# Closing lists: rows turned in blocks of 32 on VectorE by way of DRAM, and a search on the eight largest scores

## The chip, the cores and the metric

One core of a Trainium2 chip runs the kernel. The metric is the time of one execution on the device, in microseconds. Three runs of the kernel before took 1522.15, 1522.92 and 1523.63 us: median 1522.92.

## The reference

Two stages follow each other. The first mixes x [8, 2496, 256] along the sequence: a real Fourier transform over the 2496 rows, a complex 256 x 256 product with bias, soft thresholding by 0.01, and the inverse transform. Its 8 x 2496 = 19968 rows of 256 are the tokens of the second stage, in which each of eight experts takes exactly 2496 tokens:

```
logits = x @ w_gate                        # 19968 x 8
for idx in argsort(-logits.flatten()):     # greedy, largest score first
    tok, e = idx // 8, idx % 8
    if assigned[tok] >= 0 or counts[e] >= 2496: continue
    assigned[tok] = e; counts[e] += 1
out[mask_e] = relu(x[mask_e] @ w1[e]) @ w2[e]      # 256 -> 1024 -> 256, for each expert
```

## The kernel before

**Stages.** The first part (`phase_a`) does the transforms batch by batch and leaves the rows in the DRAM tensor `YD` and the logits in `LG`. While its last batches run, each expert gets an early list of 512 tokens that are sure to be its own (`Router.early`), from the first four batches. After the logits of all batches are in, eight closing lists follow (`Router.closing`, i = 0 to 7): list i finds the expert that fills up next, and the remaining 1984 of its tokens are computed. Its later tokens then move to their next best expert, so that list i+1 can only be searched once list i is found.

**Search of a closing list.** `H.m` holds each token's best score among the `no` = 8 - i experts that are open, 156 tokens to each of 128 partitions; `AG` and `EQ` say whose it is. The wanted score is the one at which the fullest expert has 2496 tokens. `count` (line 445) does one count: for each threshold and each pair of experts one VectorE instruction compares 156 columns and sums (line 454), two small ones part the two experts of a pair (lines 458, 459), and two small matmuls add up over the partitions (lines 464, 465). Lists 0 and 1 use `bisect` (line 495) behind one count: 19 halvings, and a last count, 21 rounds. Lists 2 to 6 use `search` (line 470) with three thresholds a round, 11 rounds and a last count. Each round waits for the result of the one before. List 7 takes what is left.

**A list's work.** `lists` (line 522) turns the marks into row numbers, by matmuls (line 551) and ScalarE. `Experts.load` fetches the expert's weights by the number found, with indirect DMAs of GpSimd (line 617), and splits them into two parts each. `Experts.run` (line 630) gathers tiles of 128 rows from `YD` with indirect DMAs (line 640), two tiles to a buffer `xg`. A chunk is four tiles, 512 tokens; a closing list has four chunks, 16 tiles. `xpose` (line 645) turns a chunk: for each half of the 256 columns TensorE transposes four 128 x 128 blocks into a PSUM bank (line 655), ScalarE copies the bank as the high part (line 658), and VectorE subtracts it for the low part (line 659):

```
for q in range(nt):
    t = 4 * c + q
    T.transpose(ps.t[:, 128 * q:128 * q + 128], xg[t // 2].t[:, t % 2, 128 * m:128 * m + 128], H.idn)
```

`ffn1` (line 670) multiplies with W1 in three terms, eight groups of 128 of the hidden 1024; `ffn2` (lines 689 to 692) multiplies with W2; ScalarE and VectorE merge the two parts (lines 698, 699), and GpSimd scatters the rows to the output (line 702).

**Order.** Nothing is in program order by itself: `Plan.run` simulates five queues (TensorE, VectorE, ScalarE, GpSimd and SP) with costs from the code, takes at each step the task that can start first, then the one of lower `pos`, and emits the instructions in that order. Buffers come from rings or from groups of slots. `Q`, `SLACK`, `LATE` and `GAP` are its numbers: positions of stages, allowances for waits, and transfer times. A flag `fail` is raised if the certificates of the lists don't hold; then a slow general pass (`general`) computes all again behind a `tc.If`.

## Time and profile before

| | us |
|---|---|
| median of three runs | 1522.92 |
| profiled execution | 1523.78 |
| its span, first to last instruction | 1522.0 |
| TensorE busy | 1486.1 |
| VectorE busy | 1184.8 |
| ScalarE busy | 893.2 |
| GpSimd busy | 526.4 |

PE is TensorE's matmuls, PEld its weight loads, DVE is VectorE, ACT ScalarE, POOL GpSimd and SP the queue that issues plain DMAs. A busy time is the time in which at least one instruction of the engine was under way; instructions overlap, so the mean duration of one is longer than the step from one to the next. `x4` is a number of instructions. In a name such as `b<-h_idn,yst` the output stands first; buffers are shared slots, so one tile bears many names over the run. A bracket at the end of a row is idle time before the instruction and what ended it.

### The profile page before, as it was taken

To read this page: it belongs to the slowest core of one execution; us is meant where nothing else is said; L and a number is where in the kernel's file an instruction comes from. 1 tells how busy PE (TensorE), PEld (TensorE's weight loads), DVE (VectorE), ACT (ScalarE), POOL (GpSimd) and SP (SyncE) were. 2 spreads that over 40 slices of the span, in tenths; PEclk is the share of its full clock that TensorE was granted. 3 is DMA by queue.
4 is the path that set the end of the run, shared out by engine and by line. 5 is a ranking of instruction groups with operands and counts; after the bars stand their busy time and mean duration, and the time that the engine had idled before them with its cause. 6 is when DMAs were issued, how large, how long until landed. Compare 5 with 4: busy or idle time off the path is not lost.

```text
span 1522.0 us, 33650 instructions
## 1 busy us (share of the span) xinstructions
PE 1486.1 (98%) x9511; PEld 1248.3 (82%) x9514; DVE 1184.8 (78%) x3981; ACT 893.2 (59%) x2092; POOL 526.4 (35%) x497
## 2 busy tenths in 40 slices
PE   8999999999999999999999999999999999999997
PEld 6878888888888867888777888878888888888886
DVE  5868888776898968899999999999787875543432
ACT  4668999899899785445535344363536355442331
POOL 0013424334323445312523525244433525442112
PEclk9999999999999999999999999999999999999999
DMA  5598788787777675423212212121312223220000
GB/s 199 182 298 260 231 273 269 227 279 238 239 226 246 187 222 159 155 89 119 85 42 87 66 56 91 42 93 58 99 50 86 71 68 106 68 70 29 20 25 29
DMA packets 134959, 206.98 MB, mean 136 GB/s; under 512 B 26942, under 2 KB 96747, under 8 KB 134763
## 3 DMA queue, kind: packets, MB, share of 16 engines
q1 hardware_dynamic: 114793, 146.42, 30.7%
q0 software_dynamic: 19840, 58.22, 11.9%
q8 instruction: 77, 1.26, 0.4%
q14 instruction: 119, 0.97, 0.2%
q10 hardware_dynamic: 130, 0.11, 0.0%
...
## 4 chain that ended last, share of the span: by engine, by line
PE 79%; DVE 9%; DMA 4%; ACT 4%; issue 2%; SPq 1%; POOL 0%; POOLq 0%; ACTq 0%; DVEq 0%
PE b L670 23%; PE b L689 14%; PE b L690 7%; PE b L1144 6%; PE b L1173 4%; PE b L1125 3%; PE b L1152 3%; PE pt L670 3%; PE b L1211 3%; PE b L1085 3%; DVE junk L454 2%; PE pt L689 2%; PE b L1231 2%; PE b L655 2%; PE pt L690 1%
## 5 line engine op out<-in xcount | busy, mean ns | idle before, releaser
L955 POOL TENSOR_TENSOR s2l<-s2c,s2h 120x512 fp32r<-120x512 f32 (+1 forms) x84 | 106.6, 1274 | 248.1 <-ACT s2h L952 235.8
L454 DVE SCALAR_TENSOR_TENSOR junk<-h_m,st,h_AG 128x156 bf16<-128x156 f32 (+1 forms) x472 | 155.7, 376 | 2.1
L702 POOL DMA_INDIRECT out_dram<-xTh,li x64 | 67.8, 1060 | 210.8 <-DVE xTh L699 108.7
L1144 PE MATMUL b<-wt,xTh 128*128 128x256 f32 x640 | 130.0, 300 | 3.5 <-ACT xTh L1131 3.5
L1144 PEld LDWEIGHTS b<-wt,xTh 128*128 128x128 f32 x640 | 103.1, 192 | 9.6 <-ACT xTh L1131 3.7
L1242 POOL TENSOR_TENSOR yTl<-yr,yTh 128x468 bf16<-128x468 f32 (+1 forms) x55 | 62.3, 1132 | 121.6 <-ACT yTh L1238 92.4
L702 POOL DMA_INDIRECT out_dram<-xTl,li x64 | 65.5, 1023 | 104.0 <-DVE xTl L699 54.0
L1144 PE MATMUL b<-wt,xTl 128*128 128x256 f32 x320 | 92.5, 289 | 2.9 <-DVE xTl L1134 2.4
L1125 PE MATMUL b<-FG,sh 128*128 128x128 f32 x640 | 89.8, 277 | 1.2 <-DVE sh L1106 1.2
L1125 PEld LDWEIGHTS b<-FG,sh 128*128 128x128 f32 x640 | 83.1, 191 | 8.5 <-issue 2.7
L1173 PE MATMUL b<-y,FG 64*128 64x256 f32 x640 | 80.3, 390 | 0.0
L698 ACT COPY xTh<-b 128x256 f32<-128x256 f32 x58 | 21.7, 375 | 93.0 <-PE b L690 75.9
L1173 PEld LDWEIGHTS b<-y,FG 64*128 64x128 f32 x640 | 58.3, 186 | 14.9 <-issue 3.2
L1157 DVE TENSOR_TENSOR y<-b,sx 128x512 f32<-128x512 f32 x80 | 54.8, 685 | 18.0 <-ACT sx L1155 17.5
L955 DVE TENSOR_TENSOR xl<-xt,xh 117x512 fp32r<-117x512 f32 (+1 forms) x77 | 56.6, 745 | 15.0 <-ACT xh L952 14.4
L1211 PE MATMUL b<-s2h,d 120*117 120x512 f32 (+1 forms) x168 | 66.6, 403 | 0.0
L1144 PEld LDWEIGHTS b<-wt,xTl 128*128 128x128 f32 x320 | 61.3, 191 | 5.7 <-DVE xTl L1134 4.6
L698 ACT COPY xTl<-b 128x256 f32<-128x256 f32 x74 | 27.8, 376 | 63.8 <-PE b L690 50.6
L1085 PE MATMUL b<-xh,d 117*120 117x512 f32 (+1 forms) x154 | 62.8, 421 | 1.0 <-ACT xh L952 1.0
L1152 PE MATMUL b<-wt,xTh 128*128 128x256 f32 x320 | 62.4, 287 | 0.0
L1236 DVE TENSOR_TENSOR yr<-b,yTh 128x468 f32<-128x468 f32 (+1 forms) x88 | 54.7, 622 | 7.9 <-ACT yTh L1235 4.3
L699 DVE TENSOR_TENSOR xTl<-b,xTl 128x256 f32<-128x256 f32 x74 | 30.9, 418 | 36.1 <-ACT xTl L698 33.7
...
## 6 DMA issues: line engine op xcount, KB each, us to landing
...
```

The lines of the kernel that those rows point to most:

```text
L454: v(cols + 59, p, lambda k=k: V.scalar_tensor_tensor(junk[k % 2].t[:, 0:cols], H.m[:, 0:cols], c.t[:, k // ng:k // ng + 1], ag(k % ng)[:, ...
L670: T.matmul(ps.t[:, 0:w], lhsT=W1[m].t[:, a, 128 * ft:128 * ft + 128], rhs=x_.t[:, 0:w], start=q + m == 0, stop=q + m == 3)
L689: T.matmul(ps.t, lhsT=hh.t[:, u:u + 128], rhs=W2[ft // 4].t[:, :, ft % 4], start=ft == 0, stop=False)
L690: T.matmul(ps.t[:, 0], lhsT=hl.t[:, u:u + 128], rhs=w_[0], start=False, stop=ft == 7)
L702: ins = P.indirect_dma_start(out=self.out, out_offset=bass.IndirectOffsetOnAxis(ap=oi.t[0:M, oo + t:oo + t + 1], axis=0), in_=o.t[0:M], in ...
L955: lambda: eng.tensor_tensor(lb[1](), src(), hb[1](), op=OP.subtract), [srcb, hb[0]], [lb[0]], port=True)
L1085: T.matmul(ps.t[0:M], lhsT=d1[0:k_, a, 0:M], rhs=v.t[0:k_], start=i == 0, stop=i == 2)
L1125: T.matmul(ps.t[:, :, dt, i], lhsT=sh[k // 8].t[:, k % 8, 128 * dt:128 * dt + 128], rhs=at(Ft, k), start=True, stop=True)
L1144: T.matmul(pc.t[:, c], lhsT=a.t[:, 1 - c, dt], rhs=wt[2 - c].t[:, w, dt], start=not pb and dt == 0 and a is th and w == 0, stop=(c == 1 or ...
L1152: T.matmul(pa.t, lhsT=a.t[:, 2, dt], rhs=wt[0].t[:, w, dt], start=dt == 0 and a is th and w == 0, stop=dt == 1 and a is tl)
L1173: T.matmul(ps4[i].t[:, r], lhsT=at(Gt, 2 * (p - 1 + r) + c)[h], rhs=zs[r].t[h, c], start=c == 0, stop=c == 1)
L1211: T.matmul(ps.t[0:M, gs_], lhsT=d5[0:k_, a, 0:M], rhs=v.t[0:k_, gs_], start=i == 0, stop=i == 2)
```

## The change

In all eight closing lists the rows are turned otherwise. Behind the gather of two tiles, SP writes both (256 rows) to a DRAM buffer `XG` and reads them back in four loads into `xw`: partition 32G + r gets, for each block of 32 rows, row r's columns 64G to 64G + 63. `xturn` then takes the place of `xpose`: for each half, two VectorE instructions transpose all 32 x 32 blocks of a pair (256 columns each) into an SBUF tile `xf`, ScalarE copies it as the high part, and VectorE subtracts. The 256 columns of a row now stand in another order on the partitions, so the rows of W1 are fetched with indices in that order (two more columns in `wi`). The early lists keep `xpose`.

The search is otherwise too. List 0 makes one count, five halvings and a count at the upper end, and then calls `few`. Lists 1 to 6 extrapolate from the last list's counts to two thresholds, at 0.5 and 0.85 of the way, count both in one round, take the better as upper end, and call `few`. There VectorE takes, for each open expert and partition, the eight largest scores under the upper end (three instructions of 156 columns an expert), and then 7 rounds (6 in list 0) with seven thresholds each: one comparison of 7 x no x 8 elements, one sum over the eights, one matmul over the partitions, and small instructions. A last count with all tokens stands behind it as before. `search` is gone. A few small instructions keep the counts for the next list's extrapolation.

`Q`, `SLACK` and `P1X` have new values, so the order of all queues is another; the loads of one constant (`cD5`) are planned later; two small buffers share others' places. Inside the `tc.If`, `general` is planned with numbers of its own. The diff, without the lists of numbers:

```diff
+BLOCK = (0, 1, 2, 3, 4, 5, 6, 7)
...
+SN, SR = 7, 7
+FR = 0.5, 0.85
+NEAR = 5
+WIDE = 100.0
...
+def few(K, H, pos, hi, lo, nr, no, pk):
+
+    V, v, T = K.V, K.v, K.T
+    cand, sc, D, wq = K.sb("eq", [128, 8, 8]), K.sb("lo", [128, 4, NJ]), K.sb("cno", [128, 1]), K.sb("wq", [128, SR * SN])
     low, at = lo
+    at0 = lo[1]
+    v(1, pos(), lambda: V.tensor_tensor(D.t, hi.t[:, 0:1], at0(), op=OP.subtract), [hi, low], [D])
+    v(SN * nr + 59, pos(), lambda: V.tensor_scalar(wq.t[:, 0:SN * nr], H.sq[:, 0:SN * nr], D.t[:, 0:1], None, op0=OP.mult), [H.b_sq, D], [wq])
+    c = K.sb("st", [128, 8])
+    v(SN, pos(), lambda c=c: V.tensor_scalar(c.t[:, 0:SN], wq.t[:, 0:SN], at0(), None, op0=OP.add), [wq, low], [c])
+    v(NJ + 59, pos(), lambda: V.scalar_tensor_tensor(sc.t[:, 3], H.m, hi.t[:, 0:1], H.m, op0=OP.is_lt, op1=OP.mult), [H.b_m, hi], [sc])
+    for e in range(no):
+        v(NJ, pos(), lambda e=e: V.tensor_tensor(sc.t[:, e % 3], H.ML[:, e], sc.t[:, 3], op=OP.not_equal), [H.b_ML, sc], [sc])
+        v(NJ + 59, pos(), lambda e=e: V.scalar_tensor_tensor(sc.t[:, e % 3], sc.t[:, e % 3], GONE, H.ML[:, e], op0=OP.mult, op1=OP.add), [H.b_ML, sc], [sc])
+        v(NJ, pos(), lambda e=e: V.max(cand.t[:, e], sc.t[:, e % 3]), [sc], [cand])
+    n = SN * no
+    for k in range(nr):
+        G, cn, ps = K.sb("Sme", [128, SN, 8, 8], BF), K.sb("ge0", [128, SN, 8], BF), K.psum(pk, [128, SN, 8])
+        nn, mx, g8, sm, b, c2 = K.sb("RD", [128, SN, 8]), K.sb("g8", [128, 8]), K.sb("g8", [128, 8]), K.sb("any", [128, 1]), K.sb("cno", [128, 1]), K.sb("st", [128, 8])
+        v(8 * n, pos(), lambda G=G, c=c: V.tensor_tensor(G.t[:, :, 0:no].rearrange("p j e k -> p j (e k)"), cand.t[:, None, 0:no].rearrange("p a e k -> p a (e k)").to_broadcast([128, SN, 8 * no]), c.t[:, 0:SN, None].to_broadcast([128, SN, 8 * no]), op=OP.is_ge), [cand, c], [G])
+
+        def total(G=G, cn=cn):
+            with K.nc.allow_low_precision(reason="counts up to 8"): V.tensor_reduce(cn.t[:, :, 0:no], G.t[:, :, 0:no], op=OP.add, axis=AX.X)
+        v(8 * n, pos(), total, [G], [cn], port=False)
+        K.t(.1, pos(), lambda cn=cn, ps=ps: T.matmul(ps.t[:, :, 0:no], lhsT=H.ones, rhs=cn.t[:, :, 0:no], start=True, stop=True), [cn, H.b_ones], [ps], slack=SLACK['count'])
+        v(n, pos(), lambda ps=ps, nn=nn: V.tensor_tensor(nn.t[:, :, 0:no], ps.t[:, :, 0:no], hi.t[:, None, 1:1 + no].to_broadcast([128, SN, no]), op=OP.add), [ps, hi], [nn], slack=SLACK['back'])
+        v(n, pos(), lambda nn=nn, mx=mx: V.tensor_reduce(mx.t[:, 0:SN], nn.t[:, :, 0:no], op=OP.max, axis=AX.X), [nn], [mx], port=False)
+        v(80, pos(), lambda mx=mx, g8=g8, sm=sm: V.tensor_scalar(g8.t[:, 0:SN], mx.t[:, 0:SN], float(CAP), 0.0, op0=OP.is_ge, op1=OP.add, accum_out=sm.t), [mx], [g8, sm])
+        v(59, pos(), lambda k=k, sm=sm, b=b, at=at: V.scalar_tensor_tensor(b.t, sm.t, wq.t[:, SN * k:SN * k + 1], at(), op0=OP.mult, op1=OP.add), [sm, wq, low], [b])
         low, at = b, lambda b=b: b.t
+        if k < nr - 1: v(SN, pos(), lambda k=k, b=b, c2=c2: V.tensor_scalar(c2.t[:, 0:SN], wq.t[:, SN * k + SN:SN * k + 2 * SN], b.t[:, 0:1], None, op0=OP.add), [wq, b], [c2])
         c = c2
     return b
...
+                                                                          in_offset=bass.IndirectOffsetOnAxis(ap=wi.t[:, (2 + m if block and not k else m):(2 + m if block and not k else m) + 1], axis=0)), 524e3, [wi], [r], run=4096, late=LATE['raw'])
...
+            if block and (t % 2 or t == NT - 1):
+                h, n_ = t // 2, t % 2 + 1
+                XG, w = K.dram("XG", [256, 256]), K.sb("xw", [128, 8, 2, 32])
+                K.dma(pos_g(t) + Q['xw'], lambda g=g, XG=XG, n_=n_: K.nc.sync.dma_start(XG.t[0:128 * n_].rearrange("(t p) d -> p t d", p=128), g.t[:, 0:n_]), 131e3 * n_, [g], [XG])
+
+                def ld(w=w, XG=XG, n_=n_):
+                    for G in range(4):
+                        K.nc.sync.dma_start(w.t[32 * G:32 * G + 32, 0:4 * n_].rearrange("p t m c -> p t (m c)"), XG.t[0:128 * n_].rearrange("(t r) (G c) -> G r t c", r=32, G=4)[G])
+                plan.add('SP', 1.6, pos_g(t) + Q['xv'], ld, [XG], [w], load=moved(131e3 * n_, 256, late=LATE['sp']))
+                xg[h] = w
+
+        def xturn(c, pos):
+            nt = min(4, NT - 4 * c)
+            w_ = 128 * nt
+            xT[c] = [[K.sb("xT", [128, 512], F32R) for _ in range(2)] for _ in range(2)]
+            for m in range(2):
+                h, l = xT[c][m]
+                f = K.sb("xf", [128, 512])
+                for k in range((nt + 1) // 2):
+                    w, e = xg[2 * c + k], min(8, 4 * nt - 8 * k)
+                    v(32 * e, pos + .5 * m - Q['xv2'], lambda f=f, w=w, m=m, k=k, e=e: V.transpose(f.t[:, 256 * k:256 * k + 32 * e], w.t[:, 0:e, m]), [w], [f])
+                plan.add('A', .095 + w_ / 1200, pos + .5 * m, lambda f=f, h=h: A.copy(h.t[:, 0:w_], f.t[:, 0:w_]), [f], [h])
+                v(w_, pos + .5 * m, lambda f=f, h=h, l=l: V.tensor_tensor(l.t[:, 0:w_], f.t[:, 0:w_], h.t[:, 0:w_], op=OP.subtract), [f, h], [l])
...
-        xpose(0, base - Q['xp'])
+        turn = xturn if block else xpose
+        turn(0, base - Q['xp'])
...
-            rng, r = self.rng, RR[i]
-            v(1, pos(), lambda: V.tensor_tensor(rng.t, lohi.t[:, 0:1], lohi.t[:, 1:2], op=OP.subtract), [lohi], [rng])
-            if r > 1:
-                c = search(K, H, pos, (lohi, lambda: lohi.t[:, 1:2]), rng, r, N4, CAP, no, ag, NJ, "pq", self.junk, self.acc, eqs)
...
+            hi, cur = K.sb("hi", [128, 9]), K.sb("pv", [128, 24]) if i < 6 else None
+            if i:
+                pv = self.pv
+                v(2 * no, pos(), lambda pv=pv: V.copy_predicated(pv.t[:, 8:24].rearrange("p (a e) -> p a e", a=2)[:, :, 0:no], fp.t[:, None, 0:no].bitcast(I32).to_broadcast([128, 2, no]), pv.t[:, 8:24].rearrange("p (a e) -> p a e", a=2)[:, :, no:no + 1].to_broadcast([128, 2, no])), [fp, pv], [pv])
+                q8, dl, c, P, mx, lt = K.sb("g8", [128, 8]), K.sb("any", [128, 1]), K.sb("st", [128, 8]), K.sb("P2", [128, 2, 9]), K.sb("wi", [128, 2]), K.sb("fs", [128, 2])
+                v(67, pos(), lambda pv=pv, q8=q8: V.scalar_tensor_tensor(q8.t[:, 0:no], pv.t[:, 8:8 + no], float(CAP), pv.t[:, 16:16 + no], op0=OP.subtract, op1=OP.mult), [pv], [q8])
+                v(8, pos(), lambda q8=q8, dl=dl: V.tensor_reduce(dl.t, q8.t[:, 0:no], op=OP.min, axis=AX.X), [q8], [dl], port=False)
+                v(61, pos(), lambda dl=dl, c=c, pv=pv: V.scalar_tensor_tensor(c.t[:, 0:2], H.fr, dl.t[:, 0:1], pv.t[:, 0:1].to_broadcast([128, 2]), op0=OP.mult, op1=OP.add), [dl, pv, H.b_fr], [c])
+                v(9, pos(), lambda pv=pv, hi=hi: V.tensor_copy(hi.t[:, 1:1 + no], pv.t[:, 8:8 + no]), [pv], [hi])
+                v(1, pos(), lambda pv=pv, hi=hi: V.tensor_copy(hi.t[:, 0:1], pv.t[:, 0:1]), [pv], [hi])
+                v(2, pos(), lambda c=c, P=P: V.tensor_copy(P.t[:, :, 0], c.t[:, 0:2]), [c], [P])
+                ps = count(K, H, pos, c, no, ag, NJ, "pq", self.junk, self.acc, eqs, 2)
+                for h in range(2):
+                    w_ = (ng, n2)[h]
+                    v(16, pos(), lambda ps=ps, P=P, h=h, w_=w_: V.tensor_copy(P.t[:, :, 1 + ng * h:1 + ng * h + w_], ps.t[:, 2 * ng * h:2 * ng * h + 2 * ng].rearrange("p (j g) -> p j g", j=2)[:, :, 0:w_]), [ps], [P], slack=SLACK['back'])
+                v(16, pos(), lambda P=P, mx=mx: V.tensor_reduce(mx.t, P.t[:, :, 1:1 + no], op=OP.max, axis=AX.X), [P], [mx], port=False)
+                v(2, pos(), lambda mx=mx, lt=lt: V.tensor_scalar(lt.t, mx.t, float(CAP), None, op0=OP.is_lt), [mx], [lt])
+                for j in range(2): v(9, pos(), lambda j=j, P=P, lt=lt, hi=hi: V.copy_predicated(hi.t[:, 0:1 + no], lt.t[:, j:j + 1].bitcast(I32).to_broadcast([128, 1 + no]), P.t[:, j, 0:1 + no]), [P, lt], [hi])
+                c = few(K, H, pos, hi, (lohi, lambda: lohi.t[:, 1:2]), SR, no, "pq")
...
-                c = bisect(K, H, pos, c2, KB - 3 if i < 6 else KB - 2, CAP, no, ag, NJ, "pq", self.junk, self.acc, eqs)
+                lo = bisect(K, H, pos, c2, NEAR, CAP, no, ag, NJ, "pq", self.junk, self.acc, eqs)
+                up = K.sb("st", [128, 8])
+                v(1, pos(), lambda lo=lo, up=up: V.tensor_tensor(up.t[:, 0:1], lo.t, H.wk[:, NEAR - 1:NEAR], op=OP.add), [lo, H.b_wk], [up])
+                ps = count(K, H, pos, up, no, ag, NJ, "pq", self.junk, self.acc, eqs)
+                v(8, pos(), lambda ps=ps, hi=hi: V.tensor_copy(hi.t[:, 1:9], ps.t[:, 0:8]), [ps], [hi], slack=SLACK['back'])
+                v(1, pos(), lambda up=up, hi=hi: V.tensor_copy(hi.t[:, 0:1], up.t[:, 0:1]), [up], [hi])
+                c = few(K, H, pos, hi, (lo, lambda: lo.t), SR - 1, no, "pq")
...
-            v(1, pos() + 5, lambda: V.tensor_copy(lohi.t[:, 0:1], c.t), [c], [lohi])
+            if i < 6:
...
+                self.pv = cur
...
+        v(2, pw, lambda: V.scalar_tensor_tensor(wi.t[:, 2:4], H.iE[:, 0:2], 32.0, wb.t.to_broadcast([128, 2]), op0=OP.mult, op1=OP.add), [wb, H.b_iE], [wi])
...
+    GROUPS = dict(W=(8, slots("sp8", "sh8", "FG8")), raw=(2, slots("xt")), xg=(10, G2), xw=(5, G2), xf=(2, G2), hid=(20, G2), xT=(8, G2), os=(8, slots("xTh", "xTl")),
...
+            W = X.load(base - Q['ll'], wi=wi, block=i in BLOCK)
+            X.run(CAP - EN, base, W, gi, 0, gs, oi, 0, lambda t, base=base, i=i: base + Q['gs'] * (t // 4) - (Q['gl2'] if i in BLOCK else Q['gl']) + .1 * (t % 4), block=i in BLOCK)
```

## Rows read from the trace of the kernel before

**Rows 1.** Page of the profile, part 1: busy us, share of the span, instructions.

```profile
PE 1486.1 (98%) x9511; PEld 1248.3 (82%) x9514; DVE 1184.8 (78%) x3981; ACT 893.2 (59%) x2092; POOL 526.4 (35%) x497
```

**Rows 2.** Stretches: length, busy us (instructions) by engine, granted clock, DMA share, GB/s.

```profile
740.00:1100.00 360.00, 352.52 (x1965) 292.30 (x1964) 338.42 (x1606) 161.97 (x400) 147.72 (x144) 1.00 0.23 72
1100.00:1510.00 410.00, 410.00 (x2241) 348.79 (x2241) 236.36 (x788) 166.89 (x389) 140.69 (x142) 1.00 0.18 57
```

**Rows 3.** Waits of TensorE: who for whom, us in total, times, longest.

```profile
PE b L464 <- DVE cnt L459: 7.4, 8, 1.9
...
PE b L670 <- DVE y L659: 0.2, 1, 0.2
```

**Rows 4.** Chain of waits from 1000 us on: start, us, what.

```profile
1036.11 0.44 PE b L655 x4
...
1320.35 0.44 PE b L655 x4
...
1410.54 0.44 PE b L655 x4
```

**Rows 5.** Stretches, line 655 alone: length, PE busy, PEld busy, clock, DMA, GB/s.

```profile
740.00:1100.00 360.00, 17.78 (x118) 13.55 (x116) 1.00 0.23 72
1100.00:1510.00 410.00, 20.36 (x136) 16.49 (x136) 1.00 0.18 57
```

**Rows 6.** Timeline of TensorE at 1426 us: start, us, engine, line, operation.

```profile
1426.05 0.28 PE L690 MATMUL b<-sh,xl 128*128 128x256 f32 x1
1426.17 0.38 PE L655 MATMUL b<-h_idn,yst 128*128 128x128 f32 x2
...
1426.84 0.39 PE L670 MATMUL b<-s1st,sh 128*128 128x512 f32 x1
```

**Rows 7.** Timeline of TensorE at 694 us, a counting pair.

```profile
694.07 0.39 PE L670 MATMUL b<-s1st,sh 128*128 128x512 f32 x1
694.30 0.18 PE L464 MATMUL b<-cnt,h_ones 128*128 128x4 bf16 x1
...
694.68 0.28 PE L690 MATMUL b<-FG,y 128*128 128x256 f32 x1
```

**Rows 8.** Groups of VectorE: count, busy us, mean ns, idle before.

```profile
L454 DVE SCALAR_TENSOR_TENSOR junk<-h_m,st,h_AG 128x156 bf16<-128x156 f32 x444 | 147.8, 378 | 2.0
...
L699 DVE TENSOR_TENSOR xTh<-b,xTh 128x256 f32<-128x256 f32 x58 | 24.4, 422 | 35.3 <-ACT xTh L698 33.3 <-issue 1.9
...
L484 DVE SCALAR_TENSOR_TENSOR cno<-any,wq,cno 128x1 f32<-128x1 f32 x50 | 10.9, 219 | 1.1
...
L412 DVE TENSOR_REDUCE h_m<-h_ML 128x39 f32<-128x312 f32 x4 | 3.0, 758 | 0.0
...
L414 DVE TENSOR_TENSOR eq<-h_ML,h_m 128x312 bf16<-128x312 f32 x4 | 1.9, 478 | 0.0
```

**Rows 9.** Timeline of ScalarE, the last logits leave for DRAM.

```profile
590.47 0.65 ACT L1260 COPY lgst<-b 64x234 f32<-64x234 f32 x2 [2.44 <-PE b L1253]
```

**Rows 10.** Timeline of VectorE, the logits read back are used.

```profile
604.02 0.47 DVE L410 TENSOR_TENSOR lo<-lo 128x312 f32<-128x312 f32 x1
```

**Rows 11.** Timeline of GpSimd, first gathers of lists 0 and 3.

```profile
726.41 0.96 POOL L640 DMA_INDIRECT yst<-YD,li  x1 [6.36 <-DVE junk L454]
...
1001.16 1.46 POOL L640 DMA_INDIRECT yTl<-YD,li  x1 [0.84 <-issue]
```

**Rows 12.** Timeline of TensorE, first transposes of list 0.

```profile
739.53 0.42 PE L655 MATMUL b<-h_idn,yst 128*128 128x128 f32 x2
```

**Rows 13.** Timeline of TensorE, first and last of the 22 counts of list 0.

```profile
622.26 0.18 PE L464 MATMUL b<-cnt,h_ones 128*128 128x4 bf16 x1
...
707.28 0.18 PE L464 MATMUL b<-cnt,h_ones 128*128 128x4 bf16 x1
```

**Rows 14.** DMA queues: packets, MB, share of 16 engines over the span.

```profile
q1 hardware_dynamic: 114793, 146.42, 30.7%
```

More of the change, by code (lines that the diff above doesn't have):

```diff
@@ L378, in constants @@
     dma_c(K, pos, H.pc, H.b_pc, cR[2560:2816].rearrange("(p c) -> p c", c=2), after)
-    dma_c(K, pos, H.sq, H.b_sq, row(2816 + NJ, 3 * N4), after)
+    dma_c(K, pos, H.sq, H.b_sq, row(2816 + NJ, SR * SN), after)
+    for k in range(2): v(1, pos, lambda k=k: V.memset(H.fr[:, k:k + 1], -FR[k]), [], [H.b_fr], port=False)
     v(8, pos, lambda: V.tensor_copy(H.iE, w.t[:, 0, 0:8]), [w], [H.b_iE])
@@ L467, in count @@
     return ps
-def search(K, H, pos, lo, rng, r, nk, target, no, ag, cols, pk, junk, acc, eqs=[]):
-    V, v = K.V, K.v
-    ng, n = (no + 1) // 2, r * nk
-    wq, c = K.sb("wq", [128, 3 * N4]), K.sb("st", [128, 8])
-    v(n + 59, pos(), lambda: V.tensor_scalar(wq.t[:, 0:n], H.sq, rng.t[:, 0:1], None, op0=OP.mult), [H.b_sq, rng], [wq])
-    v(r, pos(), lambda c=c: V.tensor_scalar(c.t[:, 0:r], wq.t[:, 0:r], lo[1](), None, op0=OP.add), [wq, lo[0]], [c])
-    low, at = lo
-    for k in range(nk):
-        ps = count(K, H, pos, c, no, ag, cols, pk, junk, acc, eqs, r)
-        h = 2 if no > ng else 1
-        mx, s, g8, b, c2 = K.sb("g8", [128, 8]), K.sb("any", [128, 1]), K.sb("g8", [128, 8]), K.sb("cno", [128, 1]), K.sb("st", [128, 8])
-        v(r * no, pos(), lambda ps=ps, mx=mx: V.tensor_reduce(mx.t[:, 0:r], ps.t[:, 0:h * r * ng].rearrange("p (h j g) -> p j h g", h=h, g=ng), op=OP.max, axis=AX.XY), [ps], [mx], slack=SLACK['back'], port=False)
-        v(r, pos(), lambda mx=mx, s=s, g8=g8: V.tensor_scalar(g8.t[:, 0:r], mx.t[:, 0:r], float(target), 0.0, op0=OP.is_ge, op1=OP.add, accum_out=s.t), [mx], [g8, s])
-        v(59, pos(), lambda k=k, s=s, b=b, at=at: V.scalar_tensor_tensor(b.t, s.t, wq.t[:, r * k:r * k + 1], at(), op0=OP.mult, op1=OP.add), [s, wq, low], [b])
@@ L601, in __init__, with load @@
         self.scat = []
-    def load(self, pos, e=None, wi=None):
+    def load(self, pos, e=None, wi=None, block=False):
         K, plan, v = self.K, self.K.plan, self.K.v
@@ L628, in load, with run @@
         return W1, W2
-    def run(self, n, base, W, gi, go, gs, oi, oo, pos_g, early=False):
+    def run(self, n, base, W, gi, go, gs, oi, oo, pos_g, early=False, block=False):
         K, H, plan, v = self.K, self.H, self.K.plan, self.K.v
@@ L712, in run @@
             for ft in range(HD, 8):
-                if ft == 2 and c + 1 < NC: xpose(c + 1, k)
+                if ft == 2 and c + 1 < NC: turn(c + 1, k)
                 ffn1(c, ft, k)
@@ L982, in load_consts @@
         es = sb("yr", [120, 2, 117])
-        GX.append(add_dma(-70, lambda: nc.sync.dma_start(es.t, cD5.rearrange("p (h m) -> p h m", h=2)), 112e3, [], [es], run=936, k=15, late=0))
-        plan.add('V', dve(234), 5, lambda: V.tensor_copy(d5, es.t), [es], [Bd5])
+        GX.append(add_dma(-70, lambda: nc.sync.dma_start(es.t, cD5.rearrange("p (h m) -> p h m", h=2)), 112e3, [], [es], run=936, k=15, late=12))
+        plan.add('V', dve(234), 9, lambda: V.tensor_copy(d5, es.t), [es], [Bd5])
         fg[:] = FX, GX
@@ L1493, in fft_mixing_then_moe @@
     with tc.If(nc.values_load(H.fail[0:1, 0:1], min_val=0, max_val=2 * N)):
+        kept = dict(Q), dict(SLACK)
+        Q.update(hV=0.094, hA=0, hT=0, hP=0.251, xp=14.084, f0=7.351, sc=2, k2=2.026)
+        SLACK.update(split=1.92, count=0, back=0.12, lists=0.46, os=0.13, hid=0.53)
         general(tc, nc, H, LG, YD, w1, w2, cR, out)
+        Q.update(kept[0])
+        SLACK.update(kept[1])
 _INS = ['x', 'w_r', 'w_i', 'b_r', 'b_i', 'moe_w_gate', 'moe_w1', 'moe_w2']
```

55 lines of the change are left out of this document (34 added, 21 removed).

## The prediction

> **What bounds the kernel now.** I read the shares of the page first, then three stretches side by side, TensorE's own waits, the chain of waits at the heads of the closing lists, and last the matmul timeline at one head. The page has TensorE at 98%, VectorE at 78% [rows 1]. The reader should see in the stretches that these are two regimes: from 1100 us on TensorE is busy 410.0 of 410 us and VectorE only 236.4; from 740 to 1100 TensorE misses 7.5 us of 360 and VectorE is at 338.4 of 360 (94%) [rows 2]. TensorE's waits name what is missed: 7.4 us in front of the counting matmuls of the search, for VectorE's counts; the head of a chunk (a matmul of line 670 behind its transposed rows) waited 0.2 us in the whole run [rows 3]. The chain shows the pace: from list 3 to list 6 it is (1320.35-1036.11)/3 = 94.7 us a list, and the first list with no search beside it takes 1410.54-1320.35 = 90.2 us [rows 4]. So TensorE sets the end, and VectorE's search costs it some us in lists 0 to 4.
>
> **What goes, on the path.** Eight closing lists have 16 tiles each, two halves a tile: 256 transposes (118 and 136 stand in the two stretches, two start just before 740) [rows 5]. Four of them are one head. At 1426 us a 256-column matmul starts at 1426.05 and the next work 0.12 later, at 1426.17; the first matmul behind the transposes starts 0.23 (a 512-column step) before the one at 1426.84, at 1426.61 [rows 6]. One head costs 0.44 us of TensorE time, the figure that the chain also gives it [rows 4]. 64 heads x 0.44 = **28.2 us**, on an engine that is never free there: it comes off the end in full, unless something else is late.
>
> Counting matmuls: 102 pairs in the closing lists now (21 rounds in lists 0 and 1, 11 rounds and a last count in lists 2 to 6). One pair moves the following matmul from 694.30+0.23 = 694.53 to 694.68: 0.15 us [rows 7]. Afterwards there are 20 pairs (8 in list 0, 2 in each of lists 1 to 6) and 48 single matmuls of up to 56 columns in `few` (6 rounds and 6 x 7). A single one lies between half a pair (0.08) and a pair with a longer tail (0.2); I take 0.13, nearest to the pair. 15.3 - 3.0 - 6.2 = **6.1 us** off, between 2.7 and 8.5.
>
> The waits of 7.4 us hang on the number of rounds (102 to 68) and on VectorE's load. I take half, **3.7 us**, bounds 0 and 7.4.
>
> **What comes, and what hides it.** VectorE for a list of six experts: 102 counts of 0.378 us [rows 8] become 9: -35.2. `few` adds 7 rounds x 336 elements: compared at line 414's price (0.478 for 312) 3.6 us, summed at line 412's (0.758 for 312) 5.7 us [rows 8]; candidates, 18 instructions of 156 columns at 0.378, 6.8; some 14 small ones at the 0.22 of line 484, 3.1 [rows 8]. Small instructions of a round are as many before as after, and there are fewer rounds: nothing. Turning: 16 block transposes of 256 columns a list. No row shows one; above it stands line 412's 0.758, below it two thirds of a 0.378 count (0.25, 256 columns can't be under 156); I take 0.42 of the 256-column subtraction, line 699 [rows 8]: 6.7 us (4 to 12.1). Together 25.9 in, 35.2 out: VectorE is relieved by some 9 us of about 89 a list (338.4/360 x 94.7) [rows 2, 4], and lists 5 to 7 run where it has 174 us idle. It should stay just ahead of a TensorE that now takes 94.7 - 3.5 - about 1.5 = 89.7 us a list, at 80/89.7 = 89%.
>
> The way by DRAM: SP writes each pair of gathered tiles and reads it back in four loads, 64 pairs, 320 transfers, on a queue that has nothing else to issue once the early weights are in. Latency: the nearest row of a store followed by a load is the last logits: ScalarE ends lgst at 591.12, VectorE uses what came back at 604.02, 12.9 us, an upper bound, since VectorE was at other work before [rows 9, 10]. A list's first head then stands 13 us further behind its gather. Lists 0 and 3 have 13.1 and 35.0 us from first gather to first transpose today [rows 4, 11, 12]; list 0 is the tight one. Its search takes 85 us for 22 counts (622.26 to 707.28) [rows 13], 3.9 a round; 14 rounds and 24 candidate instructions take 54 + 9 = 63, so its gathers can go 22 us earlier and the 13 are covered. For list 1 the rounds fall from 21 to 9, which covers more. If that cover is gone, the price is up to 13 us once, not per list: later lists are gathered ahead.
>
> Volume: a pair is 1024 runs of 256 B and 256 rows of 1 KB out. By bytes (queue 1 moves 146.42 MB in 30.7% of 1522 us) 0.52 MB take 1.7 us of all 16 engines, by packets (65 ns each) 5.2 us [rows 14]. 64 pairs are 107 to 333 us over 770: a DMA share of 0.14 to 0.43 on top of 0.18 to 0.23 [rows 2]. Hidden either way. The Trainium skill, "DMA: Bandwidth & Descriptors", section Specifications, speaks against this edit: a transfer wants pieces of 512 B or more, and these are 256 B. The packet-wise bound above is what that rule would look like here; by it the sum stays and the fourth rival below gains chance. No run here shows 256-byte pieces alone.
>
> ScalarE copies 64 heads from SBUF instead of PSUM: it is at 167 of 410 us [rows 2], nothing. The new buffers share 38 slots with the old ones; pairs can be read late for want of one. New small waits at 32 chunk heads: from 0 (0.2 in all today [rows 3]) to 0.5 each, one block transpose and a hand-over; I take 0.1, **+3 us**. The new order before 540 us touches no work there: 0, between -3 and +3. The code after the `If` isn't run.
>
> **Sum.** -28.2 - 6.1 - 3.7 + 3 = -35.0. The profiled execution took 1523.78 us (1.8 beyond its span), the median of the runs is 0.9 lower: 1522.92 - 35.0 = **1488 us**; its own range 1481 to 1497.
>
> **Rivals.**
> 1. *All waits go.* Both bounds on the good side: 28.2 + 8.5 + 7.4 + 0, and 1 or 2 us of the order's gaps: 1522.9 - 45.5 = 1477. For it: fewer rounds, fewer matmuls between. Against: 68 rounds still come through TensorE's queue in order.
> 2. *VectorE remains the pace of lists 0 to 3.* The relief of 9 us a list is made of bounds; with the dear ends (12.1 for turning, sums longer) it is under 4, and TensorE wants its lists 5 us sooner each. Then four lists stay at 94.7 and their 4 x 5 us are lost: 1508. For it: 94% busy today. Against: today that load costs only 7.4 us.
> 3. *Heads wait.* 0.5 us at 32 heads, 16 instead of 3: 1501.
> 4. *Slower: SP's queue.* It issues in order, so a store that waits for its gather, or a load that waits for its store to land, holds back every pair behind it. If each pair keeps the queue for its whole way, 12.9 us, a list takes 8 x 12.9 = 103 us instead of about 88, and 8 lists add 120: 1608. It decides from 88/8 = 11 us a pair. Against: only the store's landing is awaited on the queue, about half of the 12.9.
> 5. *The search doesn't do what it says:* a partition has more than eight scores in the bracket, the certificate fails and the general pass runs all over: at least eight lists of about 110 us, over 2300 us. Nothing in the profile speaks for it.
>
> **Numbers.** Forecast 0.60, rival 1 0.14, rival 2 0.10, rival 3 0.09, rival 4 0.04, rival 5 0.01, no net gain (2 and 3 together with the list-0 price) 0.02. Within 0.2% (3 us) is what a measurement here can't tell from no change. Faster 0.93, same 0.02, slower 0.05. Range 1476 to 1505: it leaves out half of rival 1's lower side, most of 2, and 4 and 5.
>
> **What would show it.** No transposes of line 655's kind after 740 us and TensorE busy about 1450; list pace about 86.5 at the end (90.2 - 3.5) and under 90 in the middle; TensorE's waits for counts under 5 us; block transposes near 0.42 us; VectorE under 90% from 740 to 1100. Waits of chunk heads on VectorE or ScalarE copies above 10 us in sum, a pace of 94 in the middle, or SP waiting on DRAM stores while TensorE idles, make it wrong.

## The result, and the profile after

The changed kernel takes **1479.05 us** (median of four runs, 1477.74 to 1479.4) against 1522.87 for the kernel before beside it: ratio **0.9711**, 95% interval [0.9694, 0.9727]. Run again later (five runs) it took 1478.09 against 1518.46, ratio 0.9744 [0.9729, 0.9758]. So its own time hardly differs between the two, but the kernel before moves by some 4 us from chip to chip, and a ratio of one chip is compared with one of another to about 0.3% only. The forecast was 1488, the range 1476 to 1505.

The profiled execution's span is 1475.9 us, 46.1 less than before. First the page's busy times [rows 1], then two stretches [rows 2], the second ending with list 7's last full tile, then TensorE's waits from 590 us on [rows 3].

```profile
PE 1449.2 (98%) x9135; PEld 1221.8 (83%) x9142; DVE 1131.0 (77%) x3234; ACT 888.7 (60%) x2092; POOL 525.2 (36%) x497
```

```profile
740.00:1100.00 360.00, 356.74 (x1907) 294.39 (x1906) 322.54 (x1228) 176.94 (x454) 166.95 (x164) 1.00 0.46 139
1100.00:1460.00 360.00, 360.00 (x1887) 308.22 (x1886) 186.66 (x456) 147.94 (x330) 113.68 (x113) 1.00 0.27 83
```

```profile
PE b L501 <- DVE ge L499: 2.2, 5, 0.6
PE pt L501 <- DVE ge L499: 0.7, 1, 0.7
PE b L710 <- issue: 0.2, 1, 0.2
```

Of the 46.1 us, 36.9 are TensorE's busy time (1486.1 - 1449.2) and 9.2 its idle time. VectorE, busy 338.4 of 360 us before, is at 322.5 (90%). TensorE's waits for counts from 590 us on are down to 2.9 us, all at `few`'s matmul (line 501); no chunk head (line 710, `ffn1` in the changed kernel) waits for its turned rows: the 0.2 us there are put down to issue, a wait for nothing that the profile shows.

The head at 1426 us shows the change at its plainest. It stands by chance at the same time as in [rows 6]; there the four transposes pushed the next ffn1 matmul to 1426.61, here it follows at once.

```profile
1426.15 0.40 PE L729 MATMUL b<-FG,xl 128*128 128x512 f32 x1
1426.39 0.28 PE L730 MATMUL b<-FG,y 128*128 128x256 f32 x1
1426.51 0.40 PE L710 MATMUL b<-y,sh 128*128 128x512 f32 x1
```

The pace, read where each list comes to its half tile (line 732; lists 2, 5, 6 and 7): (1282.17 - 1013.63)/3 = 89.5 us a list in the middle and 86.8 at the end, against 94.7 and 90.2 in [rows 4].

```profile
1013.63 0.40 PE L732 MATMUL b<-sh,yTl 128*128 128x256 f32 x2
...
1282.17 0.40 PE L732 MATMUL b<-FG,yr 128*128 128x256 f32 x2
...
1368.94 0.40 PE L732 MATMUL b<-sh,xh 128*128 128x256 f32 x2
...
1455.75 0.40 PE L732 MATMUL b<-FG,yst 128*128 128x256 f32 x2
```

On VectorE (groups: count, busy us, mean ns, idle before) the rows that answer to [rows 8] are a candidate's eight largest (line 491) and its masking (line 490), the compare and the sum of `few` for six experts, and one of many groups of block transposes:

```profile
L491 DVE MAX8 eq<-lo 128x8 f32<-128x156 f32 x35 | 11.0, 316 | 0.5
L490 DVE SCALAR_TENSOR_TENSOR lo<-lo,h_ML 128x156 f32<-128x156 f32 x35 | 11.0, 314 | 0.3
...
L496 DVE TENSOR_TENSOR Sme<-eq,st 128x336 bf16<-128x336 f32 x7 | 3.5, 500 | 0.1
L499 DVE TENSOR_REDUCE ge<-Sme 128x42 bf16<-128x336 bf16 x7 | 3.4, 492 | 0.1
...
L681 DVE STREAM_TRANSPOSE yTl<-yTh 128x256 f32<-128x256 f32 x4 | 1.7, 437 | 0.0
```

The DMA queue that carries the trips of the rows through DRAM [rows 14]:

```profile
q1 hardware_dynamic: 201833, 180.00, 39.2%
```

### The profile page after: what moved, and what is told of

Same layout as the page of the kernel before. It is cut to its first block, busy times and chain, and to the rows that moved or that the text cites. A ratio compares the mean times of both kernels' runs of the same rounds, so it can differ in the third digit from the quotient of the medians.

```text
span 1475.9 us, 32728 instructions
## 1 busy us (share of the span) xinstructions
PE 1449.2 (98%) x9135; PEld 1221.8 (83%) x9142; DVE 1131.0 (77%) x3234; ACT 888.7 (60%) x2092; POOL 525.2 (36%) x497
## 3 DMA queue, kind: packets, MB, share of 16 engines
q1 hardware_dynamic: 201833, 180.00, 39.2%
## 4 chain that ended last, share of the span: by engine, by line
PE 85%; DVE 7%; ACT 3%; DMA 2%; issue 2%; SPq 1%; POOL 0%; POOLq 0%; DVEq 0%; ACTq 0%
PE b L710 23%; PE b L729 15%; PE b L730 8%; PE b L1227 7%; PE b L1256 5%; PE b L1208 4%; PE b L1235 4%; PE b L1168 3%; PE b L1294 3%; PE pt L710 3%; PE pt L729 2%; PE b L1314 2%; PE pt L730 1%; PE b L732 1%; PE b L1336 1%
## 5 line engine op out<-in xcount | busy, mean ns | idle before, releaser
L738 ACT COPY xTh<-b 128x256 f32<-128x256 f32 x66 | 24.7, 374 | 95.2 <-PE b L730 76.6
L634 POOL DMA_INDIRECT xt<-in_moe_w_dram,wi x32 | 33.8, 1055 | 67.6 <-DVE sh L644 20.7
L739 DVE TENSOR_TENSOR xTh<-b,xTh 128x256 f32<-128x256 f32 x66 | 27.6, 418 | 38.8 <-ACT xTh L738 36.4
```

## The experiments

The change has three parts: the turning, the search, and the planner's numbers (with the constants' load; for short, the old and the new numbers). The theory was that the time is TensorE's work plus what it waits for, and that the transposes' 28 us come off in full only while VectorE has room, which the new search makes. The rival was that the parts simply add. All ratios are to the kernel before on the same chip, with 95% intervals.

### Without the turning

```diff
-BLOCK = (0, 1, 2, 3, 4, 5, 6, 7)
+BLOCK = ()
```

> The kernel after with all eight closing lists turned by TensorE again (search and order numbers stay new). Theory A, the three parts add up: 64 heads x 0.44 us come back, 1479 + 28 = 1507 (1503 to 1511), the list pace at the end back at 90.2, and TensorE's waits for counts still under 4 us. Rival B, the turning on VectorE cost some of what the search freed: without it the lists 0 to 4 run freer, waits fall below 2 us and the time is 1500 or less. Rival C, the turning gave more than its matmuls (the PSUM bank that the transposes took is free for the products): 1512 or more.

Measured 1506.2 us, 0.9906 [0.989, 0.9923], as theory A said. The turning is worth 27 to 28 us on top of the other two parts (25 to 30 by the ratios): the 28.2 of the transposes, and no new waits taken off it.

### The search alone

```diff
-                c = search(K, H, pos, (lohi, lambda: lohi.t[:, 1:2]), rng, r, N4, CAP, no, ag, NJ, "pq", self.junk, self.acc, eqs)
+                c = few(K, H, pos, hi, (lohi, lambda: lohi.t[:, 1:2]), SR, no, "pq")
...
-                c = bisect(K, H, pos, c2, KB - 3 if i < 6 else KB - 2, CAP, no, ag, NJ, "pq", self.junk, self.acc, eqs)
+                lo = bisect(K, H, pos, c2, NEAR, CAP, no, ag, NJ, "pq", self.junk, self.acc, eqs)
+                c = few(K, H, pos, hi, (lo, lambda: lo.t), SR - 1, no, "pq")
```

> The kernel before with the new search alone (TensorE turns, old numbers). Theory A: 6 us of counting matmuls and 5 us of waits go: 1512 (1509 to 1515). Rival B: only the matmuls go, the waits come back at other places because the old numbers put the rounds elsewhere: 1517. Rival C: the search alone gains nothing, since TensorE has other work in most of its waits: 1521 to 1524.

Measured 1507.91 us, 0.9915 [0.9896, 0.9934], a little below theory A's range. TensorE's busy time falls by 7.9 us (to 1478.2), its waits for sums are 2.0 us, and VectorE is down to 284.8 of 360 us from 740 to 1100.

### The numbers alone

```diff
-P1X = -7.246
+P1X = -8.145
...
+Q and SLACK as in the changed kernel, the constants cD5 loaded later
```

> The kernel before with nothing new but the order's numbers (and the general pass planned with its own, which does not run). Theory A, from the two traces: the order alone ends the logits some 4.8 us sooner, time 0.9965 to 0.998 of before (1517 to 1520). Rival B, from the search alone (0.9915) against search and numbers (0.9906): the numbers give 1 to 2 us, 0.999. Rival C: they fit the new code alone, 1.000 or more.

Measured 1540.04 us, 1.0141 [1.0124, 1.0158]: 21 us more, rival C. (`general` keeps numbers of its own here too; with the new ones its plan finds no order.) TensorE waits 15.6 us for the old search's counts alone (who for whom, us, times, longest). That the new due times were fitted to 68 rounds and not to 102 is the likely reason; no run isolates it.

```profile
PE b L464 <- DVE cnt L459: 15.6, 10, 3.2
```

### The turning alone

```diff
+            if block and (t % 2 or t == NT - 1):
...
+                plan.add('SP', 1.6, pos_g(t) + Q['xv'], ld, [XG], [w], load=moved(131e3 * n_, 256, late=LATE['sp']))
+                xg[h] = w
...
-        xpose(0, base - Q['xp'])
+        turn = xturn if block else xpose
+        turn(0, base - Q['xp'])
...
-                 wt=3, eq=1, T1=2, T2=2, pt=1, sx=2, lo=1, hs=6, ho=1,
+                 wt=3, eq=1, T1=2, T2=2, XG=64, pt=1, sx=2, lo=1, hs=6, ho=1,
```

> The kernel before with the block turning alone (old search, old numbers, four positions added, 64 DRAM buffers in place of 4 so that an order exists). Theory A: VectorE, at 94% from 740 to 1100 us, gets 6.7 us more a list and paces lists 0 to 4; 1508 to 1514, TensorE's waits from 740 to 1100 above 15 us. Rival B: the parts add up, 28 to 30 us less: 1493 (1490 to 1497), waits 7 to 9 us as before.

Measured 1508.01 us, 0.9927 [0.9908, 0.9945]: 11 us of the 28 arrive. (There are 64 DRAM buffers for the pairs because with the changed kernel's four the old numbers leave the plan no order.) The stretch and TensorE's waits say where the rest went. VectorE is busy 348.3 of 360 us (97%), TensorE misses 18.4 us in the stretch, and it waits for counts of the old search and for turned rows.

```profile
740.00:1100.00 360.00, 341.64 (x1834) 280.31 (x1833) 348.30 (x1643) 158.25 (x395) 147.18 (x139) 0.99 0.40 117
```

```profile
PE b L466 <- DVE cnt L461: 10.0, 10, 2.5
PE pt L695 <- DVE s4st L668: 3.8, 2, 3.1
PE pt L466 <- DVE cnt L461: 3.5, 2, 2.0
```

This is the mechanism of the prediction's second rival, and it holds with the old search. That the time is the rival's 1508 too is chance: the rival's sum has the new search's gain in it, this kernel has not.

### The old search in the changed kernel

```diff
-                c = few(K, H, pos, hi, (lohi, lambda: lohi.t[:, 1:2]), SR, no, "pq")
+                c = search(K, H, pos, (lohi, lambda: lohi.t[:, 1:2]), rng, r, N4, CAP, no, ag, NJ, "pq", self.junk, self.acc, eqs)
```

(and `bisect` in lists 0 and 1 as before)

> The kernel after with the old search put back (turning and numbers stay new). Theory A, VectorE short: 1500 or more, with waits of TensorE for counts above 15 us. Rival B, the parts add up: the 13 us that the search alone gave come back, 1479 + 13 = 1492 (1489 to 1495).

Measured 1541.89 us, 1.0153 [1.0136, 1.017]. TensorE stands for 26.5 us before counts of one line, and its granted clock is 0.95 in the stretch instead of 1.00:

```profile
740.00:1100.00 360.00, 321.61 (x1672) 262.13 (x1671) 341.04 (x1628) 154.40 (x383) 135.27 (x132) 0.95 0.38 111
```

```profile
PE b L466 <- DVE cnt L461: 26.5, 15, 4.6
```

Beside the numbers alone the turning gains nothing here (+1.9 us). VectorE's share doesn't explain this by itself: at 341.0 of 360 us it is below the 348.3 of the turning alone and near the 338.4 before, and yet TensorE misses 38.4 us in the stretch, against 18.4 and 7.5.

### Early lists turned by VectorE too

```diff
+EBLOCK = (0, 1, 2, 3, 4, 5, 6, 7)
...
-            W = X.load(base - Q['le'], e=e)
+            W = X.load(base - Q['le'], e=e, block=e in EBLOCK)
```

> The kernel after with the eight early lists turned on VectorE too, by the same way through DRAM (rows of W1 fetched in the same other order): 64 more transposes, 16 heads x 0.44 us, leave TensorE. Theory A: TensorE is the end there too, 1479 - 7 = 1472 (1470 to 1475). Rival B: early lists are gathered just before use while DMA is at 0.35 to 0.7 and VectorE at 92 to 95%; heads wait for the trip, and the time is 1479 to 1490. TensorE's waits on heads tell them apart: under 2 us or over 7.

Measured 1482.99 us, 0.9767 [0.975, 0.9783]: no gain, some 4 us worse than the changed kernel, although 64 more transposes are gone from TensorE. The time is rival B's and its sign is not there: TensorE waits at no head. It is busy 144.19 of the 150 us from 590 to 740, where the changed kernel has it busy all the time, and the missing time stands before two counts. One is the first count of list 0. In SP's order the load that brings the last logits back comes behind the loads of three pairs of the early lists (592.75 to 598.84), and goes out at 598.89, in the changed kernel at 588.48.

```profile
588.48 0.59 SPq L410 DMA_DIRECT2D h_ML<-LG  x1
```

```profile
596.71 2.13 SPq L673 DMA_DIRECT2D yTh<-XG  x4
598.89 0.59 SPq L411 DMA_DIRECT2D h_ML<-LG  x1
```

```profile
609.63 0.16 PE L472 MATMUL b<-cnt,h_ones 128*128 128x4 bf16 x1 [2.69 <-DVE cnt L467]
```

VectorE uses these logits at 603.87 instead of 597.55, and the first count is done at 609.63 instead of 606.31. The other wait, 3.12 us, is for a sum of `few` at 737.21. With only early lists 4 to 7 so:

```diff
-EBLOCK = (0, 1, 2, 3, 4, 5, 6, 7)
+EBLOCK = (4, 5, 6, 7)
```

> The changed kernel with the early lists 4 to 7 also turned by VectorE (the early lists 0 to 3 stay with TensorE). Done for all eight early lists it took the time from 0.9711 to 0.9767, with TensorE waiting 6.0 us at the few's matmuls and VectorE at 143.8 of 150 us from 590 to 740 us. Theory (VectorE's room in that stretch decides): the early lists 4 to 7 run in the same stretch, so half of the transposes saved (4 lists x 8 x 0.44 us / 4 per list, a few us at most) against half of the load: ratio 0.970 to 0.975, no better than the changed kernel by more than 0.2%. Rival (there is room for half of it): 0.967 to 0.970, faster than the changed kernel by the transposes saved.

1479.58 us, 0.973 [0.9716, 0.9744]: as the changed kernel. VectorE is busier here from 590 to 740 (144.7 us, against 143.8 with all eight), TensorE misses 2.4 us instead of 5.8, and the load of the logits goes out at 589.49. So it isn't VectorE's share that makes the version with all eight slower; the late logits are the cause that the two traces show for the first wait, and no run isolates them. No version beat the changed kernel.

### Each block transpose twice

```diff
-                    v(32 * e, pos + .5 * m - Q['xv2'], lambda ...: V.transpose(...), [w], [f])
+                    for _ in range(2):
+                        v(32 * e, pos + .5 * m - Q['xv2'], lambda ...: V.transpose(...), [w], [f])
```

> The changed kernel with every block transpose done twice into the same tile: 128 more VectorE transposes of 0.43 us, 55 us in all, some 6.9 us a list; nothing else differs. VectorE was busy 322.5 of the 360 us from 740 to 1100 us and gets 27.5 us more there: 350, or 97%, the share that it had in the kernel with the turning and the old search. Theory (TensorE collects its 28 us only while VectorE has room; the new search makes the room): close to the limit again, the lists lose some of the gain: 1484 to 1495 us (ratio 0.975 to 0.982), the loss in the lists before 1100 us, TensorE waiting for counts there. Rival (VectorE's share does not matter by itself, only the length of the chain of dependent search steps on the counts, which is not longer here): as the changed kernel, ratio 0.970 to 0.973. Second rival (VectorE already paces): all 55 us are paid, above 1520 us (ratio 1.0).

Measured 1483.84 us, 0.9753 [0.9739, 0.9767]: at the near end of what the theory allowed, and by the ratio not apart from the 0.9744 of the changed kernel's second run. The trace leans to the theory: the span is 6.7 us longer (1482.6), VectorE at 339.3 of 360 us (94%, not the 97% expected), TensorE misses 7.8 us of the stretch instead of 3.3, and the waits for `few`'s sums are 6.4 us instead of 2.9. The added transposes, 42 us of VectorE's busy time in all (1173.2 against 1131.0), cost 1 to 6 us of the end: most of them still find room.

```profile
PE b L501 <- DVE ge L499: 4.6, 5, 1.3
PE pt L501 <- DVE Sme L496: 1.8, 1, 1.8
```

### A second trip through DRAM

```diff
-                K.dma(pos_g(t) + Q['xw'], lambda ...: K.nc.sync.dma_start(XG..., g.t[:, 0:n_]), 131e3 * n_, [g], [XG])
+                K.dma(pos_g(t) + Q['xw'], lambda ...: K.nc.sync.dma_start(XF..., g.t[:, 0:n_]), 131e3 * n_, [g], [XF])
+                K.dma(pos_g(t) + Q['xw'], lambda ...: K.nc.sync.dma_start(XG..., XF...), 131e3 * n_, [XF], [XG])
```

> The changed kernel with a second stop in DRAM: the gathered pair is written to a first DRAM buffer, copied to a second one, and read from there. One more DMA of 256 KB for each of 32 pairs, 8 MB both ways, and a wait more in SP's queue, at the same due times. In the changed kernel a store's issue and its read's issue lie some 6 us apart (741.35 and 747.34 us), so the second copy adds about as much to the trip. Theory (the trip lies under the lead of the gathers, and SP's queue has room): within 0.2% of the changed kernel, ratio 0.969 to 0.973, no waits of VectorE on the block transposes. Rival (the trip is only just covered, or SP's waits hold back the weight loads and the stores of early rows behind them): each list's heads wait some 3 us, 8 x 3 = 24 us, ratio 0.985 or more, with VectorE or TensorE waiting at the first transposes of each list.

(There are 64 pairs, not 32, and 16.8 MB more each way.) Measured 1482.03 us, 0.9744 [0.9731, 0.9758]: outside the 0.969 to 0.973 expected, far from the rival's 0.985, and the same as the changed kernel's own second run. In us it is 3 to 4 more than the changed kernel, on a chip where the kernel before took 2.3 us more as well; a loss of that size can't be told from none. The trace shows no wait for a pair on VectorE and none at a head on TensorE: covered, with a DMA share of 0.56 in the stretch.

```profile
740.00:1100.00 360.00, 354.18 (x1894) 292.79 (x1893) 323.12 (x1221) 177.04 (x454) 167.52 (x163) 1.00 0.56 167
```

### Four lists of eight

```diff
-BLOCK = (0, 1, 2, 3, 4, 5, 6, 7)
+BLOCK = (4, 5, 6, 7)
```

> The changed kernel with only lists 4 to 7 turned by VectorE; lists 0 to 3 are turned by TensorE again, as all eight were in the kernel with the new search and numbers alone (ratio 0.9906, 27 us more than with all turned). Theory (with the new search each list's transposes come off in full wherever it stands, 32 x 0.11 = 3.5 us a list): half of the gain, 0.9800 to 0.9825. Rival (lists 0 to 3 are still held by VectorE, so that their turning gained nothing or lost): nearly all of the gain stays, 0.9711 to 0.975. Rival on the other side (the gain lies in the early lists alone): 0.985 or more.

Measured 1490.7 us, 0.98 [0.9786, 0.9814]: about half of the turning's gain. By the spans of the profiled executions the last four lists bring 14.8 us (1503.8 to 1489.0) and the first four 13.1 (1489.0 to 1475.9). So lists beside a search (0 to 3) give nearly as much for a transpose as lists with VectorE half idle: with the new search VectorE no longer holds the first four back by more than some us.

### The old numbers, and the changed kernel again

> The changed kernel itself, unaltered, for a comparison on one chip with the next kernel. Ratio 0.9694 to 0.973; if it comes near 0.9744, the 0.3% by which the kernel with two trips stood above it was the chip and not the second trip.

This is the second run told of at the top. Its ratio, 0.9744, is above the range expected; so the 0.3% by which the kernel with two trips stood above the first run are no sign against the second trip.

```diff
-P1X = -8.145
+P1X = -7.246
...
+Q, SLACK and the load of cD5 as before
-                 wt=3, eq=1, T1=2, T2=2, XG=4, pt=1, sx=2, lo=1, hs=6,
+                 wt=3, eq=1, T1=2, T2=2, XG=64, pt=1, sx=2, lo=1, hs=6,
```

> The changed kernel with the old planner numbers (due times, slacks and load of the constants as before) and room for 64 DRAM buffers, so the block turning and the search on 8 scores without the replanning. It is the one combination of the three parts not yet timed. Theory (the new search frees VectorE, and with that the turning's 28 us come off whatever the numbers; the numbers are worth little, 1.4 us from the search alone 1507.9 to search and numbers 1506.2): 1 to 6 us above the changed kernel, ratio 0.972 to 0.976. Rival (the old numbers place the turning's DMAs and block transposes badly, so that the replanning is what lets it in): the turning gains only some 11 us, as it did on top of the old search, ratio 0.980 to 0.985, with waits of TensorE at chunk heads or counts in lists 0 to 4. On the third side (the old numbers suit better): at or below the changed kernel.

Measured 1489.41 us, 0.981 [0.9795, 0.9824]; on the same chip 11.3 us above the changed kernel. The theory fell here: with the turning the numbers are worth 11.3 us, where they gain 1.7 beside the search alone. The rival's ratio came, and so did its sign, a wait at a chunk head beside counts, though the turning still gains 16 to 18 us and not 11. Nearly all of the loss stands in one place. In TensorE's timeline the early lists end at 749.75; until 762.77 nothing is there but five of list 1's sums in `few`, 3 us apart, because list 0's first chunk is not ready.

```profile
749.47 0.28 PE L730 MATMUL b<-FG,s1st 128*128 128x256 f32 x1
749.90 0.19 PE L501 MATMUL b<-ge,h_ones 128*128 128x49 bf16 x1 [0.15 <-DVE ge L499]
...
761.77 0.20 PE L501 MATMUL b<-ge,h_ones 128*128 128x49 bf16 x1 [2.70 <-DVE ge L499]
762.77 0.80 PE L710 MATMUL b<-FG,sp 128*128 128x512 f32 x1 [0.80 <-ACT FG L682]
```

The rows of GpSimd, SP, VectorE and ScalarE give that chunk's way: first gather at 740.04, the two pairs written from 744.30 and 747.79, the second read back from 750.33, the two pairs turned from 758.71 and 761.63, the first half copied at 762.10.

```profile
740.04 0.96 POOL L657 DMA_INDIRECT s2h<-YD,li  x1 [4.55 <-PE pt L730]
```

```profile
744.30 0.37 SPq L664 DMA_DIRECT2D XG<-s2h  x1
747.79 0.37 SPq L664 DMA_DIRECT2D XG<-yTl  x1
...
750.33 1.87 SPq L668 DMA_DIRECT2D yTh<-XG  x4
```

```profile
758.71 0.43 DVE L681 STREAM_TRANSPOSE xl<-s4st 128x256 f32<-128x256 f32 x1
...
761.16 0.56 DVE L499 TENSOR_REDUCE ge<-Sme 128x49 bf16<-128x392 bf16 x1
761.63 0.43 DVE L681 STREAM_TRANSPOSE xl<-yTh 128x256 f32<-128x256 f32 x1
```

The trip was over well before the turning. These are the packets, MB and share of 16 engines of the DMA queues from 753 to 754 us, and from 754.5 to 758:

```profile
q1 hardware_dynamic: 290, 0.07, 32.1%
```

```profile
q0 software_dynamic: 96, 0.27, 23.8%
q14 instruction: 1, 0.01, 0.7%
```

Queue 1, which carries the trips, moves its last bytes of these pairs before 754 us and nothing from 754.5 to 758, and VectorE's own waits ahead of the transposes last at most 0.05 us each. So the second pair's trip, from 747.79, took about 6 us. After 754 both pairs lie ready, and VectorE works on list 1's search and on row numbers, which stand before the block transposes in its order. Of the gap from 749.75 to 762.77 the trip has at most 4.3 us; the other 8.8 lie behind it, and the two block transposes of the first half and ScalarE's copy are about 1.5 us of them. ScalarE's row shows what it waited for, 11.95 us long:

```profile
762.10 0.62 ACT L682 CAST FG<-xl 128x512 fp32r<-128x512 f32 x1 [11.95 <-DVE xl L681]
```

In the changed kernel the first gather of list 0 goes out at 708.54 and its first matmul starts at 745.59, without a gap:

```profile
708.54 0.99 POOL L657 DMA_INDIRECT yTh<-YD,li  x1 [1.09 <-ACT ajunk L573]
```

```profile
745.47 0.28 PE L730 MATMUL b<-FG,y 128*128 128x256 f32 x1
745.59 0.40 PE L710 MATMUL b<-s1st,sp 128*128 128x512 f32 x1
```

So the way from gather to matmul has 37 us in the changed kernel and takes 22.7 with the old numbers, where it is the last thing that TensorE waits for: the rows are gathered late, and VectorE turns them late. The search alone gathers as late (744.9) and loses nothing by it (TensorE's gaps after 590 us are 2.3 us in sum): where TensorE turns the rows, the way to the first matmul has neither the trip nor VectorE's turning in it. Of the 11.3 us, 9.0 are idle time: TensorE misses 12.30 us of the stretch, against 3.26 in the changed kernel. The rest is the clock, below.

```profile
740.00:1100.00 360.00, 347.70 (x1832) 288.80 (x1832) 303.20 (x1064) 166.62 (x415) 152.15 (x148) 0.98 0.41 122
```

All eight combinations (ratio):

| | old search | new search |
|---|---|---|
| old numbers, turned by TensorE | 1 | 0.9915 |
| old numbers, turned by VectorE | 0.9927 | 0.981 |
| new numbers, turned by TensorE | 1.0141 | 0.9906 |
| new numbers, turned by VectorE | 1.0153 | 0.9711, 0.9744 |

The parts don't add. The turning is worth 27 to 28 us with both others, 16 to 18 with the search alone (1507.91 to 1489.41, or 0.9915 to 0.981), 11 with neither, and nothing with the numbers alone. By the profiled executions, in the order search, numbers, turning, the span falls by 14.6, 3.6 and 27.9 us, and TensorE's busy time by 7.9, 3.0 and 26.0.

## Why the prediction was right, point by point

What bounds the kernel and what the change takes off it came as forecast: TensorE sets the end, its transposes come off in full, VectorE is just relieved enough. The amount was small: 35 us forecast, 43.8 measured between the medians. The result lies in the stated range by 3 us and below the sum's own range (1481 to 1497) by 2.

- **Transposes, 28.2 us: right.** Taken out of the changed kernel they cost 27 to 28 (1506.2 against 1478.1 and 1479.05), half of them give about half.
- **Counting matmuls, 6.1: right.** A pair moved the next work by 0.15 us [rows 7]. A single one of `few` moves it by 0.14: from 1029.69 to 1030.29 are 0.60 us for two 512-column steps of 0.23.

```profile
1029.69 0.40 PE L710 MATMUL b<-s1st,sh 128*128 128x512 f32 x1
1029.93 0.19 PE L501 MATMUL b<-ge,h_ones 128*128 128x21 bf16 x1
1029.97 0.48 PE L710 MATMUL b<-y,sh 128*128 128x512 f32 x1
1030.29 0.39 PE L710 MATMUL b<-FG,sh 128*128 128x512 f32 x1
```

  So 102 pairs x 0.15 - 20 x 0.15 - 48 x 0.14 = 5.6. TensorE's busy time fell by 36.9 - 28.2 = 8.7 beside the transposes, and by 7.9 with the search alone; the 2 to 3 us above 5.6 stay unexplained (some records are missing, and ends are modelled).
- **Waits for counts, 3.7 of 7.4: a little small.** TensorE's gaps from 590 to 1100 us fell from 8.5 to 3.3, by 5.2. Fewer rounds left less than half of the waits.
- **New waits at chunk heads, +3: wrong, measured 0.** This is the step most off in its mechanism: the trace names 0.2 us at line 710, put down to issue. Even with a second trip TensorE waits at no head.
- **The order before 540 us, 0: wrong, measured -4.8.** TensorE's last logits are at 584.96 instead of 589.78, and their copy (ScalarE) at 585.47 instead of 590.47 [rows 9]. TensorE's idle time before 590 us fell with it, from 18.5 to 13.8 us.

```profile
585.47 0.65 ACT L1343 COPY lgst<-b 64x234 f32<-64x234 f32 x2 [1.30 <-PE b L1336]
```

  Which part does that stays open: TensorE's last logits are at 588.8 with the search alone, but at 582.8 to 585.6 in all other kernels, those with the old numbers and the turning among them.
- **VectorE.** Forecast 89% in the stretch, measured 90%. Block transposes at 0.42 us: 0.425 to 0.44. Dear and cheap ends met: the sum over 336 columns was cheaper (0.492 for 0.758), a candidate's pass too (0.314 for 0.378).
- **The trip by DRAM, covered: right, and on a condition.** The prediction named it: list 0 is the tight one, up to 13 us once. The old numbers show a price of that size at that place, 11.3 us, but it isn't the trip's: a trip of about 6 us, not the 12.9 of the bound, ends there before 754 us, and most of the gap comes from the block transposes' place behind list 1's rounds in VectorE's order, which the prediction had no term for. It is the replanning that gathers list 0's rows 31.5 us earlier (708.54 instead of 740.04) and turns them in time; the search alone didn't bring the 22 us that the prediction counted on, as with the old numbers the first gather is later than before (726.41). Which of the new numbers does it wasn't tried.
- **DMA, 107 to 333 us of all engines for 64 pairs: at the low end.** Queue 1 took 39.2% of 1475.9 - 30.7% of 1522.0 = 111 us more for 33.6 MB more, 1.74 us a pair, which is the price by bytes. The rule of the Trainium skill that was weighed ("DMA: Bandwidth & Descriptors", Specifications: pieces of 512 B or more) doesn't show here: the trips, with half their bytes in pieces of 256 B, moved at 33.6 MB / 111 us = 302 GB/s, near the queue's rate before (146.42 MB / 467 us = 313).

The sum was -35 and the span moved by -46.1 (the profiled execution before was slower than its median, the one after faster): of the 11 us missing 3 are from the heads, 4.8 from the early order, 1.5 from the waits and 2.6 from the rest of TensorE's busy time (8.7 for 6.1), to about 1 us. They happened to have one sign; that the result still fell within the range is luck in part. The first rival (all waits go, 1477) came nearest to the time, and for its reason as far as 5.2 of 8.5 us. The second (VectorE paces lists 0 to 3) is what the turning does without the new search. The third (heads) is excluded by the waits. The fourth (SP's queue) is excluded for the closing lists by the second trip: one more transfer and one more wait for each pair, and no loss that can be told from the spread. Its mechanism is real all the same: with all early lists turned by VectorE the last logits were read back 10.4 us later, behind pairs in SP's queue.
